# Weight rounding paced by products instead of by turns, with three chunks rounded in earlier turns, in a fused attention and feed-forward kernel

## The chip, the cores and the metric

The kernel runs on one core of a Trainium2 chip. The metric is the device time of one execution in microseconds (us). The engines are named as the profile names them: PE is TensorE (matmuls and transposes), PEld its weight loads, DVE is VectorE, ACT is ScalarE, POOL is GpSimd, SP is SyncE, which issues most DMAs. Each engine works through its own instructions in the order in which the program issues them, and waits at an instruction until what that instruction needs is there.

## The reference

Four batches, eight heads, 768 positions, 64 numbers per head. Every query and every key is assigned to the nearest of 16 centroids of its head; a query attends only to keys of its own cluster. The result goes through a feed-forward block of 512 to 2048 to 512 with a quick GELU.

```python
mask = q_assign[:, :, :, None] == k_assign[:, :, None, :]
scores = np.where(mask, scale * np.matmul(q, k.transpose(0, 1, 3, 2)), -1e9)
attn = softmax(scores)
x = (attn @ v).transpose(0, 2, 1, 3).reshape(B * S, H * D)
h = x @ w_in
out = ((h * (1.0 / (1.0 + np.exp(-1.702 * h)))) @ w_out).astype(np.float32)
```

The attention inputs are 32-bit floats. The two weight matrices come as 64-bit floats, and the chip computes in 32 bits, so the kernel has to round them first. That rounding is what the change moves.

## The kernel before, in words

**Turns.** Attention is cut into 96 turns, counted by t in the loop at L643. A turn works on two key tiles (128 keys against 384 queries, for two heads at a time). Three turns make a group: one pair of heads, one half of the queries. Turns 0 to 23 are batch 0, 24 to 47 batch 1, and so on. In a turn the program issues: the scores on PE (L420); for batch 0 the mask as a second small matmul (L434); the exponentials on ACT (L445); from batch 1 on the mask as a multiplication on DVE (L456, four per turn); the sums of the exponentials on POOL (L469); the products with the values of the turn before on PE (L481). When t leaves the remainder 1 on division by 3 (from turn 4 on) the turn also normalises a group: two PE matmul pairs (L493), then a reciprocal (L496) and a multiplication (L498) on DVE.

**Preparation.** The next head pairs are prepared in pieces that a table hands to turns (L611 to L621): transposes of q and k (`prep_turn`, PE L298, copied out by ACT L303), `prep_near` (PE L312, ACT L318), `prep_assign` (PE L323, then five DVE instructions L329 to L344 or L352), and `prep_hot` in batch 0 (PE L385, then a DVE copy L390 and an ACT copy L392) or `prep_spread` later. `prep_assign(1)`, `(2)` and `(3)` are in turns 1, 3 and 6, `prep_hot(1)`, `(2)` and `(3)` in turns 2, 4 and 7; `prep_assign(4)` is in turn 21 and `prep_assign(5)` in turn 24.

**Three banks.** Most small PE results go to one pool of three PSUM banks (`bank()`, L107, with bufs=3 at L91), handed out in rotation in program order. A fourth request waits until the readers of the first are done. Transposes, `prep_near`, `prep_assign`, `prep_hot` (two banks), the normalisation, and the products of the feed-forward block all ask here; so does a chunk that is rounded in PSUM.

**Rounding.** The weights are 32 chunks of 128x512 64-bit numbers (512 KB each): 16 of w_in, then 16 of w_out. `rounding` (L165) is a generator with four steps, each a DVE instruction: L174, L178, L181 and L185. With the first step it asks for the load of the chunk two further on (`load_w`, an SP DMA, three buffers). With the fourth step it also issues the final addition L189, either on POOL as two halves of 128x256 or on DVE as one instruction of 128x512, and `check_w` on ACT (L219, L222, each with an accumulator read). `step()` runs one step, `round_next()` a whole chunk, `round_to(n)` whatever is missing to n chunks, and `advance(n)` up to n steps as long as the counter `steps[0]` is above 0. The arguments that `round_next` hands on say where the sum is built and which engine adds: `(True, nc.vector)` is in PSUM and on DVE, nothing is in SBUF and on POOL.

**The second block in attention.** After turn 13 the first half of batch 0 is complete, and its feed-forward block is worked off between the turns: 16 products of the first layer (`first`, PE L554, each followed by a tanh on ACT, L517, and a multiplication on DVE, L518, which frees the bank), then 12 of the second (`second3`, PE L527). The counter `owed` (L673 to L691) takes 1.6 products per turn: one in turns 14, 16, 19, 21, 24 and 26, two in the others up to turn 28. I number the first 16 from 0. `first` calls `advance(3)` between its matmuls and its tanh; the loop calls `advance(2)` after every product, `advance(2)` before the masks, `advance(1)` once in the middle and once after every preparation piece.

**Rounding before the change.** One chunk each in turns 0, 2, 5, 8, 9, 11, 12 and 13, in turns 0, 2 and 13 at the end of the turn. From turn 14 on each turn adds 8 steps to the counter.

Of the kernel before, what the change touches and what calls it, by code (L numbers as in the profile page):

```python
# [18 lines left out]
def kernel(  # L19
    tc: tile.TileContext,  # L20
    q: bass.AP,
    k: bass.AP,
    v: bass.AP,
    centroids: bass.AP,
    moe_w_in: bass.AP,
    moe_w_out: bass.AP,
    out: bass.AP,
):

    args = (q, k, v, centroids, moe_w_in, moe_w_out, out)
    bad = fast(tc, *args)
    with tc.If(bad > 0):
        general(tc, *args)
# [3 lines left out]
def fast(  # L39
# [26 lines left out]
    nc = tc.nc  # L66
# [8 lines left out]
    HP = H // 2  # L75
# [123 lines left out]
    def step(*how):  # L199

        if not now and w_done[0] < NW:
            now.append(rounding(*(how or (False, nc.gpsimd))))
        if now:
            n = w_done[0]
            next(now[0])
            if w_done[0] > n:
                now.clear()

    def round_next(*how):
        n = w_done[0]  # L210
        while w_done[0] == n < NW:
            step(*how)
# [201 lines left out]
    def scores(u):  # L414
        g, kt = divmod(u, NJ)
        p, h = split(g)
        ps = ps_s.tile([P, 2, 512], FP32, name="s")
        for a in range(2):
            rows = slice(a * D, (a + 1) * D)
            nc.tensor.matmul(out=ps[:, a, 0:HALF],  # L420
                             lhsT=T[p, 1][rows, kt * P:(kt + 1) * P],
                             rhs=T[p, 0][rows, h * HALF:(h + 1) * HALF],
                             start=True, stop=(p >= HP))
        s_of[u] = ps[:, :, 0:HALF]

    def part(u):

        g, kt = divmod(u, NJ)
        p, h = split(g)
        if p >= HP:  # L430
            return
        for a in range(2):
            r = 32 * (2 * (p % 2) + a)
            nc.tensor.matmul(  # L434
                out=s_of[u][:, a, :],
                lhsT=hots[p // 2, 1][r:r + NC, kt * P:(kt + 1) * P],
                rhs=hots[p // 2, 0][r:r + NC, h * HALF:(h + 1) * HALF],
                start=False, stop=True)

    def exps(u):  # L440
        p, h = split(u // NJ)
        s = s_of[u]
        if p < HP:
            A_of[u] = ap.tile([P, 2, HALF], FP32, name="A")
        nc.scalar.activation(out=A_of[u] if p < HP else s, in_=s, func=AF.Exp,  # L445
                             scale=SCALE)

    def mask(u):

        g, kt = divmod(u, NJ)  # L450
        p, h = split(g)
        s = s_of.pop(u)
        if p >= HP:
            A_of[u] = ap.tile([P, 2, HALF], FP32, name="A")
            for a in range(2):
                nc.vector.scalar_tensor_tensor(  # L456
                    out=A_of[u][:, a, :],
                    in0=qcode[p][:, a, h * HALF:(h + 1) * HALF],
                    scalar=code[p][:, kt % NH, 1, kt // NH, a:a + 1],
                    in1=s[:, a, :], op0=ALU.is_equal, op1=ALU.mult)  # L460
        A = A_of[u]
        if kt == 0:
            return
        if kt == 1:
            sum_of[g] = ap.tile([P, 2, HALF], FP32, name="sum", bufs=2)


        for a in range(2) if w_done[0] < NW else (slice(0, 2),):
            nc.gpsimd.tensor_tensor(  # L469
                out=sum_of[g][:, a],  # L470
                in0=(A_of[u - 1] if kt == 1 else sum_of[g])[:, a],
                in1=A[:, a], op=ALU.add)

    def values(u):
        g, kt = divmod(u, NJ)
        p, h = split(g)
        if kt == 0:
            o_of[g] = ps_o.tile([P, 512], FP32, name="o")
        A = A_of.pop(u)
        for a in range(2):  # L480
            nc.tensor.matmul(out=o_of[g][a * D:(a + 1) * D, 0:HALF],  # L481
                             lhsT=v_in[p][:, a, kt, :], rhs=A[:, a, :],
                             start=(kt == 0), stop=(kt == NJ - 1))
        if kt == NJ - 1:
            O_of[g] = xp.tile([P, HALF], FP32, name="x")
            nc.scalar.copy(O_of[g], o_of.pop(g)[:, 0:HALF])  # L486

    def normalise(g):

        sm = sum_of.pop(g)  # L490
        ps = bank()
        for a in range(2):
            nc.tensor.matmul(out=ps[a * D:(a + 1) * D, 0:HALF], lhsT=twos,  # L493
                             rhs=sm[:, a, :], start=True, stop=True)
        rec = recs[g] = short()
        nc.vector.reciprocal(out=rec, in_=ps[:, 0:HALF])  # L496
        x = xT_of[g] = O_of.pop(g)
        nc.vector.tensor_tensor(out=x, in0=x, in1=rec, op=ALU.mult)  # L498
        if g % HP == HP - 1 and g < 2 * HP:
            (half_ffn, ffn)[g // HP].extend((ffn_half, ffn_tiles)[g // HP]())  # L500
# [3 lines left out]
    def check(g):  # L504


        rec = recs.pop(g)
        nc.scalar.activation(out=rec, in_=rec, func=AF.Copy,
                             accum_out=row_sums[:, 0, g:g + 1])
        nc.scalar.activation(out=rec, in_=rec, func=AF.Relu, bias=top[:, 0:1],  # L510
                             scale=-2.0 * LIMIT * LIMIT,
                             accum_out=row_sums[:, 1, g:g + 1])
# [23 lines left out]
    steps = [0]  # L536

    def advance(n):
        while n and steps[0] > 0:
            step()  # L540
            steps[0] -= 1
            n -= 1
# [65 lines left out]
    TG = NJ // 2  # L608
    TB = 2 * HP * TG

    prep_at = {}  # L611
    for p in range(1, NPAIR):
        b, hp = divmod(p, HP)
        for i in range(2 if p == 1 else 0, len(PREP)):
            if p == 1:
                t = (i - 2) // 2
            elif b == 0:
                t = (hp - 2) * TG + 1 + i // 2
            else:
                t = b * TB + TG * hp - (7, 7, 6, 6, 4, 3, 2)[i]  # L620
# [5 lines left out]
    def prep(p, i):  # L626
        if i == 0 and p:
            load_v(p)
        PREP[i](p)
        if i in (1, 3) and loads:  # L630
            load_qk(*loads.popleft())
# [2 lines left out]

    pace = {t: 1 for t in (0, 2, 5, 8, 9, 11, 12, 13)}
    owed = 0.0
    for p, i in [(0, i) for i in range(6)] + [(1, i) for i in range(2)]:
        prep(p, i)  # L640
# [2 lines left out]
    for t in range(NT + 2):  # L643
        us = range(2 * t, 2 * t + 2) if t < NT else ()
        for u in us:
            scores(u)
        if t == 0:
            prep(0, 6)
        for u in us:
            part(u)  # L650
        for u in us:
            exps(u)
        second_half = t >= TB // 2
        if t > TB // 2 + 1:
            steps[0] += 8
        late = t <= 2 or t == TB // 2 + 1
        if pace.get(t) and not late:
            round_next(*((True, nc.vector) if t > HP * TG // 2 else ()))
        advance(2)
        if recs:  # L660
            check(*recs)
        for u in us:
            mask(u)
        work = sorted(prep_at.get(t, ()), key=lambda w: PREP[w[1]] != prep_near)
        while work and PREP[work[0][1]] == prep_near:
            prep(*work.pop(0))
        if 1 <= t <= NT:
            for u in range(2 * t - 2, 2 * t):
                values(u)

        kept = NF // 2 if t < NT - 3 else NF // 4
        todo = half_ffn or (ffn if len(ffn) > kept else ())
        if not todo:  # L673
            owed = 0.0
        elif half_ffn:
            owed += rate
        else:
            owed += 0.65 if t < NT - 3 else 1.0
        g = (t - 2) // TG if t >= 2 and (t - 2) % TG == TG - 1 else None
        if g is not None and second_half:  # L680
            normalise(g)
        advance(1)
        for p, i in work:
            prep(p, i)
            advance(1)
        if g is not None and not second_half:
            normalise(g)
        while owed >= 1 and todo:
            todo.popleft()()
            owed -= 1  # L690
            advance(2)  # L691
        if pace.get(t) and late:
            round_next(t > 2, nc.vector)
    check(*recs)
    qcode.clear()
    att.close()
# [648 lines left out]
```

## Time and profile before

| what | value |
|---|---|
| median of 6 runs | 1028.02 us (1027.31 to 1030.46) |
| the profiled execution | 1027.92 us, of which the span from first to last instruction is 1026.1 us |
| PE busy | 990.5 us, 97% of the span |
| DVE busy | 676.9 us, 66% |
| POOL busy | 445.2 us, 43% |
| ACT busy | 373.6 us, 36% |
| granted clock of PE, mean | 0.991 |
| turn 0 starts, turn 14 starts, turn 26 starts | 11.12, 75.77, 197.45 us |

The busy shares are means over stages that differ. The change touches turns 0 to 26 alone, the first fifth of the span, so it has to be read there: which engine has no idle time left in a stretch of turns, and which instruction PE waits for.

### The profile page before, as it was taken

The page shows a single profiled execution, that of the slowest core. Times are in us where ns is not written, and L with a number is a line of the kernel's source. Part 1 is how long each engine was busy: PE and PEld are TensorE (multiplying, and loading weights), DVE is VectorE, ACT ScalarE, POOL GpSimd, SP SyncE. Part 2 cuts the span into 40 slices and gives each one's busy share as a digit, 9 for nine tenths or more (in the row PEclk, how much of TensorE's full clock was granted, in tenths as well). Part 3 has the DMA queues.
Part 4 walks back from the last instruction along what each step waited for, and adds up shares of the span by engine and source line. Part 5 has one row for each costly group of instructions (what it writes and reads, how often), then busy time and mean ns, then how long its engine had stood idle before and what let it go on. Part 6 is the DMA issues. An engine that isn't in the chain of part 4 may idle for free.

```text
span 1026.1 us, 12628 instructions
## 1 busy us (share of the span) xinstructions
PE 990.5 (97%) x4574; PEld 580.6 (57%) x4574; DVE 676.9 (66%) x1054; ACT 373.6 (36%) x761; POOL 445.2 (43%) x373
## 2 busy tenths in 40 slices
PE   7999888999999999999999999999999999999997
PEld 3434444344554445543454355688755888656886
DVE  4699999745676877777877677734477535576431
ACT  5677667333455454555444222200122100222000
POOL 3687877623665566556666677400022000120000
PEclk9999999899999999999999999999999999999999
DMA  8413544210022200221000000000000000000000
GB/s 227 129 63 124 170 143 148 74 45 19 1 62 70 71 27 7 56 70 32 19 2 1 11 1 1 0 21 21 21 1 0 1 21 21 21 0 1 21 22 24
DMA packets 66118, 45.25 MB, mean 44 GB/s; under 512 B 52096, under 2 KB 60032, under 8 KB 66048
## 3 DMA queue, kind: packets, MB, share of 16 engines
q1 hardware_dynamic: 65904, 44.33, 14.7%
q8 instruction: 38, 0.62, 0.3%
q14 instruction: 32, 0.26, 0.1%
q10 hardware_dynamic: 144, 0.03, 0.0%
HBM read 38.04 MB, written 6.31 MB: 43 GB/s over the span
## 4 chain that ended last, share of the span: by engine, by line
PE 85%; DVE 11%; ACT 2%; issue 1%; DMA 0%; SPq 0%; DVEq 0%; ACTq 0%
PE b L842 21%; PE b L785 21%; PE s L420 12%; PE o L481 11%; PE m L527 8%; PE m L584 5%; PE m L298 2%; PE m L493 2%; DVE e L185 2%; PE m L554 1%; DVE e L181 1%; DVE short L496 1%; PE m L312 1%; DVE w_in L178 1%; DVE w_out L178 1%
## 5 line engine op out<-in xcount | busy, mean ns | idle before, releaser
L469 POOL TENSOR_TENSOR sum<-sum,A 128x768 f32<-128x768 f32 (+1 forms) x162 | 244.2, 1521 | 126.9 <-DVE A L456 117.1
L456 DVE SCALAR_TENSOR_TENSOR A<-qb,code,s 128x384 f32<-128x384 uint8 x288 | 157.5, 608 | 88.9 <-ACT s L445 53.8
L420 PE MATMUL s<-T,T 64*128 64x384 f32 x768 | 153.0, 511 | 2.3 <-DVE A L456 0.4
L445 ACT ACTIVATE s<-s 128x768 f32<-128x768 f32 x144 | 109.0, 793 | 104.9 <-PE s L420 92.5
L481 PE MATMUL o<-A,inv 128*64 128x384 f32 x768 | 145.1, 499 | 1.1 <-ACT x L486 1.1
L723 POOL TENSOR_TENSOR W<-w_in 128x256 f32<-128x256 f32 x24 | 17.7, 739 | 260.8 <-PE b L785 259.1
L776 DVE TENSOR_TENSOR G<-b,G 128x384 f32<-128x384 f32 x168 | 93.4, 556 | 48.1 <-PE b L785 41.3
L517 ACT ACTIVATE th<-G 128x384 f32<-128x384 f32 x96 | 50.2, 523 | 163.2 <-DVE G L776 102.8
L776 DVE TENSOR_TENSOR y<-b,y 128x256 f32<-128x256 f32 x54 | 22.1, 423 | 130.0 <-PE b L842 93.8
L420 PEld LDWEIGHTS s<-T,T 64*128 64x128 f32 x768 | 65.0, 185 | 74.4 <-issue 33.2
L785 PE MATMUL b<-x,w_in 128*128 128x384 f32 x288 | 101.2, 486 | 0.0
L481 PEld LDWEIGHTS o<-A,inv 128*64 128x64 f32 x768 | 46.6, 136 | 85.2 <-issue 81.5
L469 POOL TENSOR_TENSOR sum<-A 128x768 f32<-128x768 f32 (+1 forms) x41 | 62.0, 1522 | 59.9 <-DVE A L456 34.0
L496 DVE RECIPROCAL short<-m 128x384 f32<-128x384 f32 x32 | 81.6, 2551 | 9.0 <-PE m L493 8.0
L518 DVE SCALAR_TENSOR_TENSOR G<-th,G 128x384 f32<-128x384 f32 x96 | 68.5, 714 | 16.8 <-ACT th L517 14.2
L785 PEld LDWEIGHTS b<-x,w_in 128*128 128x128 f32 x288 | 54.7, 190 | 37.9 <-issue 0.5
L785 PE MATMUL b<-x,W 128*128 128x384 f32 x192 | 70.5, 490 | 0.0
L842 PE MATMUL b<-Z,G 128*128 128x256 f32 x288 | 65.1, 379 | 0.0
L527 PE MATMUL m<-w_out,g 128*128 128x512 f32 x120 | 60.0, 619 | 4.2 <-DVE short L332 3.7
L842 PE MATMUL b<-w_out,G 128*128 128x256 f32 x288 | 63.6, 379 | 0.0
L842 PEld LDWEIGHTS b<-w_out,G 128*128 128x128 f32 x288 | 54.6, 190 | 8.1
L842 PEld LDWEIGHTS b<-Z,G 128*128 128x128 f32 x288 | 54.7, 190 | 7.4
(126 smaller groups left out, 1343.9 us busy)
## 6 DMA issues: line engine op xcount, KB each, us to landing
raw<-in_moe_w_in_dram SPq DMA_DIRECT2D x16, 512.0 KB, 4.7
raw<-in_moe_w_out_dram SPq DMA_DIRECT2D x16, 512.0 KB, 3.4
in<-in_q_dram SPq DMA_DIRECT2D x32, 192.0 KB, 3.6
in<-in_k_dram SPq DMA_DIRECT2D x32, 192.0 KB, 3.0
inv<-in_v_dram SPq DMA_DIRECT2D x16, 384.0 KB, 4.2
out_dram<-y SPq DMA_DIRECT2D x15, 256.0 KB, 2.4
qb<-line SPq DMA_DIRECT2D x12, 192.0 KB, 3.3
out_dram<-y SPq DMA_DIRECT2D x18, 128.0 KB, 1.8
```

What stands on the lines that cost most here:

```text
L420: nc.tensor.matmul(out=ps[:, a, 0:HALF], lhsT=T[p, 1][rows, kt * P:(kt + 1) * P], rhs=T[p, 0][rows, h * HALF:(h + 1) * HALF], start=True, ...
L445: nc.scalar.activation(out=A_of[u] if p < HP else s, in_=s, func=AF.Exp, scale=SCALE)
L456: nc.vector.scalar_tensor_tensor(out=A_of[u][:, a, :], in0=qcode[p][:, a, h * HALF:(h + 1) * HALF], scalar=code[p][:, kt % NH, 1, kt // NH ...
L469: nc.gpsimd.tensor_tensor(out=sum_of[g][:, a], in0=(A_of[u - 1] if kt == 1 else sum_of[g])[:, a], in1=A[:, a], op=ALU.add)
L481: nc.tensor.matmul(out=o_of[g][a * D:(a + 1) * D, 0:HALF], lhsT=v_in[p][:, a, kt, :], rhs=A[:, a, :], start=(kt == 0), stop=(kt == NJ - 1))
L496: nc.vector.reciprocal(out=rec, in_=ps[:, 0:HALF])
L518: nc.vector.scalar_tensor_tensor(out=g, in0=t, scalar=1.0, in1=h, op0=ALU.add, op1=ALU.mult)
L527: nc.tensor.matmul(out=ps[:, 0:DM], lhsT=g, rhs=w_out[:, f, :], start=(f == 0), stop=(f == NF - 1))
L584: nc.tensor.matmul(out=ps[:, f % 2 * P:(f % 2 + 1) * P], lhsT=w_in[:, c, f * P:(f + 1) * P], rhs=xT[c][:, n * P:(n + 1) * P], start=(c == ...
L776: nc.vector.tensor_tensor(out=o, in0=p, in1=a, op=ALU.add)
L785: nc.tensor.matmul(out=ps[:, 0:HALF], lhsT=a[:, c], rhs=x(c), start=(c == 0), stop=(c == 1))
L842: nc.tensor.matmul(out=ps[:, 0:DN], lhsT=a(f // 4)[:, f % 4], rhs=z(f), start=(f == 0), stop=(f == FB - 1))
```

## The change

Rounding before turn 14 covers three more chunks, in turns 1, 3 and 6, at the end of the turn. In turns 0 to 6 all of these now use the default form, with the addition on POOL; before, turns 0 and 2 added on DVE. From turn 14 on the counter no longer takes 8 steps per turn. It takes 4 with every product, at the moment the product is started, and 2 at the start of a turn that doesn't normalise (t % 3 != 1).

```diff
-    pace = {t: 1 for t in (0, 2, 5, 8, 9, 11, 12, 13)}
+    first, last = (5, 8, 9, 11, 12), (0, 1, 2, 3, 6, TB // 2 + 1)
...
         second_half = t >= TB // 2
-        if t > TB // 2 + 1:
-            steps[0] += 8
-        late = t <= 2 or t == TB // 2 + 1
-        if pace.get(t) and not late:
-            round_next(*((True, nc.vector) if t > HP * TG // 2 else ()))
+        dense = t > TB // 2 + 1
+        how = (True, nc.vector) if t > HP * TG // 2 else ()
+        if t in first:
+            round_next(*how)
+        if dense and t % TG != 1:
+            steps[0] += 2
         advance(2)
...
         while owed >= 1 and todo:
+            steps[0] += 4 if dense else 0
             todo.popleft()()
             owed -= 1
             advance(2)
-        if pace.get(t) and late:
-            round_next(t > 2, nc.vector)
+        if t in last:
+            round_next(*how)
```

Here TB is 24, TG is 3 and HP is 4, so `TB // 2 + 1` is turn 13 and `t > HP * TG // 2` means t > 6.

## The prediction

> **What bounds the kernel where the change acts.** I looked first at the busy times by stage, cutting the span where turns begin: turns 8 to 13 (52.6 to 75.8), 14 to 17, 18 to 21, 22 to 24, and 25 to 31. The columns are the length, then the busy time of PE, PEld, DVE, ACT and POOL, the granted PE clock, DMA share and GB/s.
>
> ```profile
> 52.60:75.80 23.20, 21.84 (x131) 8.10 (x130) 21.84 (x23) 18.63 (x42) 20.32 (x21) 1.00 0.22 69
> 75.80:113.50 37.70, 32.94 (x140) 15.56 (x138) 36.63 (x45) 24.56 (x58) 29.73 (x29) 0.95 0.45 138
> 113.50:152.80 39.30, 35.62 (x164) 17.30 (x163) 37.84 (x49) 25.39 (x59) 32.39 (x31) 0.96 0.46 144
> 152.80:186.70 33.90, 30.13 (x127) 14.17 (x126) 31.48 (x43) 19.57 (x46) 23.07 (x24) 0.90 0.50 148
> 186.70:257.60 70.90, 70.66 (x282) 30.61 (x281) 36.47 (x55) 24.75 (x50) 27.66 (x20) 1.00 0.13 37
> ```
>
> From turn 8 to turn 24 DVE is busy 93 to 97% of the time and PE only 87 to 94%; from turn 25 on PE never waits (70.66 of 70.90). So DVE bounds turns 8 to 24 and PE all that follows. The waits of PE in turns 14 to 24 say where DVE makes itself felt (us in total, times, longest):
>
> ```profile
> PE m L554 <- DVE x L518: 4.8, 2, 3.3
> PE m L527 <- DVE short L332: 3.7, 1, 3.7
> PE m L554 <- DVE short L332: 3.5, 1, 3.5
> ```
>
> In order of time: 1.43 in turn 16 (product 3 needs the bank of product 1), 3.34 in turn 17 (product 4, bank of product 3), 3.52 in turn 21 (product 11, bank of `prep_assign(4)`), 3.68 in turn 24 (first product of layer two, bank of `prep_assign(5)`). After 180.56, when the last one ends, PE waits for nothing. **The date of L332 in turn 24 is therefore what the first stage costs.** The third view is DVE's own timeline back from there:
>
> ```profile
> 53.16 2.56 DVE L496 RECIPROCAL short<-m 128x384 f32<-128x384 f32 x1 [0.92 <-ACT qb L392]
> ...
> 147.92 0.56 DVE L332 TENSOR_TENSOR short<-m,best 128x384 bf16<-128x384 f32 x1
> ...
> 156.92 2.56 DVE L496 RECIPROCAL short<-m 128x384 f32<-128x384 f32 x1 [1.37 <-PE m L493]
> ...
> 179.86 0.56 DVE L332 TENSOR_TENSOR short<-m,best 128x384 bf16<-128x384 f32 x1
> ```
>
> Between 53.16 and 180.42 DVE has one pause over 0.15 us, the 1.37 before the reciprocal of turn 22, where it waits for PE. So three links in a row: DVE without pause to L332 of turn 21 (148.48), PE from there to the normalisation of turn 22, DVE without pause to L332 of turn 24.
>
> **What one rounding step costs.** DVE's groups in turns 14 to 24 (busy us, mean ns):
>
> ```profile
> L185 DVE SCALAR_TENSOR_TENSOR e<-raw,e 128x512 f32<-128x512 uint32 x24 | 22.1, 922 | 0.7
> L178 DVE SCALAR_TENSOR_TENSOR w_out<-raw,w_out 128x512 int32<-128x512 int32 x15 | 17.0, 1131 | 0.5
> L181 DVE TENSOR_SCALAR e<-w_out 128x512 int32<-128x512 int32 x14 | 11.0, 784 | 1.1
> L174 DVE TENSOR_SCALAR w_out<-raw 128x512 int32<-128x512 int32 x15 | 10.0, 664 | 0.0
> ```
>
> That is 3.50 per chunk, and 3.38 for the eight w_in chunks: 0.86 per step. It depends on POOL. With POOL idle the four steps of a chunk took 2.25 (84.18 to 86.43); beside POOL's sums they took 4.06 (26.58 to 30.64, in turn 2). The ends for a step are 0.56 and 1.02.
>
> **Part 1: turns 0 to 7.** Each of the three new chunks stands on DVE behind `prep_assign` and ahead of the copy L390 of the next turn's `prep_hot`. In turns 2 and 4 that copy holds a bank that the second transpose of the same turn needs: three banks, `prep_hot` takes two, the first transpose the third. Turn 2 on DVE, then on PE:
>
> ```profile
> 23.88 0.65 DVE L344 TENSOR_TENSOR hot<-code,rank 128x384 bf16<-128x384 f32 x1
> 25.99 0.56 DVE L390 COPY qb<-m 64x768 bf16<-64x768 bf16 x1 [1.47 <-PE m L385]
> ```
>
> ```profile
> 26.22 0.93 PE L298 MATMUL m<-ident,in 128*128 128x128 f32 x6
> ```
>
> The second transpose starts about 26.65, just behind the copy's end at 26.55. With a chunk from 24.53 on, and POOL held by the chunk's own addition (so near the low price, 2.4), the copy runs 26.9 to 27.5: PE waits **0.85** (0.75 at 2.25; 2.5 at 4.06). In turn 4 L344 ends at 34.75 and the transpose starts at 36.3; the copy would end at 37.7, and 0.5 later since POOL, delayed in turn 2, now works beside L335 (1.09 in turn 7 instead of 0.36): **1.9** (1.25 to 3.8). In turn 7 no transpose follows, but DVE's reciprocal does; of the chunk's 2.4 the pauses there swallow 0.61 and 0.92, which leaves DVE **0.8** late (0.7 to 2.5). PE is then 2.75 late and DVE 3.55 (bounds 2.7 and 8.8). As DVE has no pause from 53.16 on, all 3.55 goes into the chain. Nothing excludes that POOL is silent throughout, but a gain there is excluded: the additions that leave DVE in turns 0 and 2 (2 times 0.69) ended before DVE had to wait for PE anyway (4.21 and 0.62).
>
> What else these chunks issue: ACT's `check_w`, 1.7 to 1.8 each, falls into ACT's pauses of 1.29, 1.95 and 1.81 before the exponentials of turns 2, 4 and 7; uncovered it would cost 0.5. Three loads of 512 KB come earlier, where DMA is busy 66% (turns 0 to 4) and 44% (5 to 7); the chunk they load is needed two chunks later. SP's queue has a free buffer each time, so the q and k loads behind are not held up; else PE would wait for them, up to the 3 to 5 us of a load. POOL gets ten more halves by turn 6 and runs some 4 us late in turn 7; the exponentials of turn 9 need its sums, which had 3.9 to spare. I count 0; each us beyond 4 would count one.
>
> **Part 2: turns 14 to 24.** 21 chunks are left instead of 24, so 12 steps fewer, about 10 us of DVE. But they must come off ahead of the two L332 to count. Following the calls of `advance` through the turns gives the steps issued from turn 14 on, before and after the change:
>
> | ahead of | before | after |
> |---|---|---|
> | L518 of product 1 (turn 15) | 14 | 11 |
> | L518 of product 3 (turn 16) | 22 | 19 |
> | L332, turn 21 | 59 | 56 |
> | L496, turn 22 | 66 | 60 |
> | L332, turn 24 | 83 | 80 |
> | end | 96 | 84 |
>
> So 9 of the 12 go away behind the last L332, under PE work that never waits: worth 0 (uncovered they would be 7.7). To L332 of turn 21: 3 steps fewer, **-2.6** (-1.7 to -3.1). To the reciprocal of turn 22 PE leads, which keeps the -2.6; the 3 further steps saved here only lengthen DVE's pause. From there to turn 24's L332 it is 17 steps before and 20 after: **+2.6** (1.7 to 3.1). Sum 0, within 1.4 either way. Other order changes (steps ahead of a gelu, POOL's L189 ahead of sums in turns 15, 18, 21 and 24) move a step's mean price; 0.04 on 56 steps is 2.2 either way.
>
> [...] Matmuls after waits of 3.34 to 3.68 run slow (eight L554 take 4.21 after the wait of turn 21 and 2.85 after the 1.43 of turn 16; sixteen take 7.12 in turn 17 and 5.43 in turn 20), and the clock in these stages is 0.90 to 0.96. [...] L174 takes 0.41 to 1.22. [...]
>
> **Sum.** 3.55 + 0 = 3.55 on the profiled execution's 1027.92 (0.10 below the median of the runs): 1031.5 us.
>
> **Rivals.** *Even* (0.22): POOL is silent beside the new chunks (+2.7) and turn 21's wait falls low enough to leave the matmuls at speed (4.21 to 2.85, -1.4): 1029.2. For it: the low price was measured; against: turn 21's bank is freed no sooner relative to PE. *Faster* (0.16): DVE's backlog, not its total, is the trouble. With each gelu 1 to 8 steps nearer its product, steps get cheaper, and the waits of turns 16, 17 and 21 vanish (-8.3) with two slow stretches (-1.7, -1.4): 1027.9 + 3.6 - 11.4 = 1020.1. It needs a mean step under 0.76 in turns 14 to 21 (5.7 us more off 56 steps). For it: 0.56 is possible; against: POOL's work there is the same. *Dearer* (0.10): the new chunks run beside POOL's sums (8.8): 1036.7, or 1038.4 if turn 4's wait then slows the matmuls as turn 17's did (7.12 less 5.43). That the steps don't come as planned is excluded by the count: `round_to` never finds a chunk missing.
>
> **Chances.** The forecast's own case has 0.52 (1030 to 1034). About 0.2% (2 us) is what a measurement of this kernel can tell from no change. Slower 0.62 (forecast and dearer), same 0.22, faster 0.16. The range, 1025 to 1036.5, leaves out most of *faster* and half of *dearer*.
>
> **What would show it.** Right: PE waits before L298 for DVE's L390 in turns 2 and 4 (0.85, 1.9); turn 14 starts near 78.5; the wait before L527 in turn 24 grows to about 6; turn 26 starts near 201; no wait in turn 16. Wrong: no L390 wait (part 1), or turn 24's L332 earlier than 182 (part 2: the price of a step).

## The result and the profile after

The changed kernel takes 1028.08 us (median of 37 runs) where the kernel before takes 1029.3 us (75 runs, among them later ones than the six of the prediction). The ratio is 0.9986, with a 95% interval of 0.9982 to 0.9991: faster by about 1.4 us. I had forecast 3.5 us slower, and had put at 2 us what can be told from no change; over this many runs 1.4 is clear of the noise. The profiled execution has a span of 1025.3 us against 1026.1.

First the busy times of the changed kernel by stage, cut at the same turns as before (length; PE, PEld, DVE, ACT, POOL; PE clock, DMA share, GB/s):

```profile
56.43:80.46 24.03, 22.00 (x129) 8.26 (x129) 22.96 (x27) 18.86 (x42) 22.32 (x22) 1.00 0.28 88
80.46:117.33 36.87, 32.92 (x140) 15.60 (x138) 35.69 (x43) 23.03 (x54) 29.83 (x29) 0.95 0.43 134
117.33:156.53 39.20, 35.41 (x162) 17.28 (x161) 37.30 (x46) 23.80 (x55) 31.74 (x31) 0.96 0.49 150
156.53:184.98 28.45, 27.66 (x125) 13.23 (x124) 24.65 (x34) 19.34 (x46) 20.74 (x22) 1.00 0.43 123
184.98:255.95 70.97, 70.73 (x282) 30.66 (x281) 36.79 (x56) 23.14 (x46) 25.70 (x16) 1.00 0.13 37
```

The stages from turn 8 to turn 21 are as long as before, within 0.9 us. The turns ahead of them are longer: turn 8 starts at 56.43 instead of 52.56, with turn 0 at 11.15 and 11.12. The gain is in the fourth line: turns 22 to 24 take 28.45 instead of 33.90, and PE's clock there is 1.00 instead of 0.90. What PE waits for, up to turn 26 (us in total, times, longest):

```profile
...
PE m L554 <- DVE x L518: 3.9, 1, 3.9
PE m L298 <- DVE qb L390: 3.2, 2, 2.3
PE m L554 <- DVE short L332: 2.9, 1, 2.9
...
PE m L527 <- ACT T L303: 0.6, 1, 0.6
```

The two waits for L390 are new and are those I had forecast, 0.91 and 2.25. The wait of turn 16 is gone, also as forecast. But the wait of 3.68 before L527 for L332 in turn 24, which I had forecast to grow to 6, is missing. PE in that turn, before and after, and DVE after:

```profile
180.56 2.04 PE L527 MATMUL m<-w_out,g 128*128 128x512 f32 x2 [3.68 <-DVE short L332]
182.40 4.33 PE L527 MATMUL m<-w_out,x 128*128 128x512 f32 x6
```

```profile
181.35 1.13 PE L527 MATMUL m<-w_out,g 128*128 128x512 f32 x2 [0.64 <-ACT T L303]
182.31 2.74 PE L527 MATMUL m<-w_out,x 128*128 128x512 f32 x6
```

```profile
184.89 0.56 DVE L332 TENSOR_TENSOR short<-m,best 128x384 bf16<-128x384 f32 x1
```

The product starts at 181.35 and L332, for which it had waited before, runs only at 184.89. The product no longer needs the bank that L332 reads. The built programs list a bank for every tile: of the 201 requests to the three-bank pool the first 78 get the same bank in both kernels, and then they part, exactly at this product.

```
request, turn             before  after
76  prep_assign(5)  24       0      0
77  transpose       24       1      1
78  transpose       24       2      2
79  product (L527)  24       0      1
80  normalisation   25       1      2
81  prep_spread     25       2      0
82  prep_near       26       2      0
83  transpose       26       1      2
84  transpose       26       2      0
```

So the banks are not handed out in strict rotation, as I had written; the tile framework chooses them when the kernel is built, and the changed rounding, the only thing that differs, was enough to change its choice. That became the theory: **the gain is the other bank, and the rounding itself costs about what it saves.** The rival: the pacing made the gain, as the diff suggests. To separate them, the runs below hand out the banks from a list. The edit is the same in all of them, with the digits of the one or the other program ("old banks", "new banks"):

```diff
-    ps_m = ctx.enter_context(tc.tile_pool(name="ps_m", bufs=3, space=PS))
+    ps_m = [ctx.enter_context(tc.tile_pool(name=f"ps_m{i}", bufs=1, space=PS)) for i in range(3)]
...
-        return ps_m.tile([P, 512], FP32, name="m")
+        return ps_m[banks.popleft()].tile([P, 512], FP32, name="m")
```

### The profile page after: what moved, and what is told of

Read it like the earlier page. It is cut to its first block, busy times and chain, and to the rows that moved or that the text cites. A ratio compares the mean times of both kernels' runs of the same rounds, so it can differ in the third digit from the quotient of the medians.

```text
span 1025.3 us, 12630 instructions
## 1 busy us (share of the span) xinstructions
PE 989.2 (96%) x4574; PEld 579.6 (57%) x4574; DVE 676.0 (66%) x1052; ACT 373.2 (36%) x761; POOL 446.5 (44%) x375
## 4 chain that ended last, share of the span: by engine, by line
PE 84%; DVE 12%; ACT 2%; issue 1%; DMA 0%; POOL 0%; DVEq 0%; ACTq 0%
PE b L844 21%; PE b L787 21%; PE s L420 11%; PE o L481 10%; PE m L527 8%; PE m L584 5%; DVE e L185 2%; PE m L298 2%; PE m L493 2%; DVE e L181 1%; PE m L554 1%; DVE short L496 1%; PE m L312 1%; DVE w_out L178 1%; DVE w_out L174 1%
## 5 line engine op out<-in xcount | busy, mean ns | idle before, releaser
L527 PE MATMUL m<-w_out,g 128*128 128x512 f32 x120 | 59.1, 611 | 1.1 <-ACT T L303 1.1
```

Source lines behind the costliest of these rows:

```text
L527: nc.tensor.matmul(out=ps[:, 0:DM], lhsT=g, rhs=w_out[:, f, :], start=(f == 0), stop=(f == NF - 1))
```

## Experiments

**1. The changed kernel with old banks.**

> The changed kernel, with the PSUM banks of the small pool handed out as in the kernel before. Theory (bank): the changed kernel gained only because the first product of layer two in turn 24 came to lie in the bank of a transpose instead of that of prep_assign(5). Put back, PE waits in turn 24 for DVE's L332 again, about 4.7 us (185.45 less 180.71), and its matmuls run slow after it, about 2.1 to 2.7 more: turn 25 starts about 7 us later than in the changed kernel, and the kernel takes about 1035 us, slower than before. Rival (pacing): the steps tied to products made the gain; then turn 24 stays as in the changed kernel and the time at about 1028.

Measured: 1034.83 us, ratio 1.0057 (1.0044 to 1.0070). PE in turn 24:

```profile
186.92 2.05 PE L527 MATMUL m<-w_out,g 128*128 128x512 f32 x2 [4.88 <-DVE short L332]
188.76 3.91 PE L527 MATMUL m<-w_out,x 128*128 128x512 f32 x6
```

The wait is back (4.88), the eight matmuls take 5.75 instead of 3.70, and turn 25 starts 14.70 after turn 24 instead of 8.41. In this run 122 further requests have another bank than in the changed kernel. But from turn 10 to the end of attention no other turn differs from the changed kernel's by more than 0.25, so it is this bank that counts, and handing out from a list costs nothing that shows. (Turns 4 to 9, ahead of the first other bank, differ by 0.6 in sum; see the last section.) The theory holds: without the other bank the change is a loss of nearly 6 us.

**2. The kernel before with new banks.**

> The kernel before, with the banks handed out as in the changed kernel; nothing of the rounding is changed. Theory (bank): in turn 24 the wait of 3.68 for L332 goes, a short one for ACT's copy stays (about 1.3), the matmuls run at speed; turn 25 starts 4 to 5 us sooner and the kernel takes 1024 to 1025.5 us. Rival (pacing): no effect, 1029, since the rounding still falls due by turn.

Measured: 1028.45 us, ratio 0.9990 (0.9981 to 0.9998). Half a miss. Turn 24 shrinks as expected, from 13.92 to 9.10, with a wait of 1.33 for ACT. But turn 26 grows from 8.05 to 10.49: PE waits 2.32 for ACT's L318, and ACT had been stuck (PE's wait first, then ACT):

```profile
PE m L298 <- ACT short L318: 2.3, 1, 2.3
```

```profile
195.94 0.71 ACT L219 ACTIVATE raw<-raw 128x512 f32<-128x512 f32 x1 [6.99 <-DVE w_out L178]
...
200.21 0.46 ACT L318 COPY short<-m 128x384 f32<-128x384 f32 x1
```

This is `check_w` of the last chunk. It alone writes its result over the raw chunk (the others use the tile of the last chunk as scratch), so ACT waits until DVE has read the raw data in L178; behind it stand the exponentials, the checks L508 and L510 and the copy L318, whose bank a transpose of turn 26 needs. With PE early, the rounding that is left late does have a price. (In this profile turns 21 and 22 are also longer, by 1.26 and 0.3; see the last section.)

**3. and 4. Each half of the change alone, old banks.** The edits against the changed kernel (3) and against the kernel before (4):

```diff
-        if dense and t % TG != 1:
-            steps[0] += 2
+        if dense:
+            steps[0] += 8
...
-            steps[0] += 4 if dense else 0
```

```diff
-        if t > TB // 2 + 1:
-            steps[0] += 8
+        dense = t > TB // 2 + 1
+        if dense and t % TG != 1:
+            steps[0] += 2
...
+            steps[0] += 4 if dense else 0
             todo.popleft()()
```

> Only the first half of the change: the three early chunks (and the additions of turns 0 and 2 on POOL), 8 steps per turn from turn 14 on, banks as before. Theory: PE waits before L298 for L390 in turns 2 and 4 as in the changed kernel (0.9 and 2.3), turn 14 starts 4.7 us late, 83 steps stand ahead of turn 24's L332 as before, so its date is about 5 us late, and nothing gives this back: about 1034 us. Rival (the early chunks relieve the dense turns): turn 24's L332 no later than before, 1029 or less.

> Only the second half of the change: 8 chunks before turn 14 as before, 24 after it, 4 steps per product and 2 per turn that does not normalise, banks as before. Theory: turn 14 starts as before; 80 steps instead of 83 ahead of turn 24's L332, which comes 0 to 2.6 us sooner; PE still waits for it, 3.5 us or more, and runs slow after it: 1027 to 1029 us. Rival (pacing): the waits of turns 16, 17, 21 and 24 shrink together, 1024 us or less.

Measured: 3 has a ratio of 1.0061 (1.0048 to 1.0074), about 6 us slower, as the theory said; the wait of turn 24 is 3.65. 4 takes 1035.9 us, ratio 1.0071 (1.0058 to 1.0084), which neither side expected. Its turn 24 is as expected (wait 4.91), but turn 26 takes 13.68 instead of 8.05. PE's waits from there on:

```profile
PE m L527 <- POOL w_out L189: 3.2, 2, 2.8
```

Without the early chunks the slower pacing issues 88 steps to the end of turn 25, not 96. That leaves two chunks over (I had counted three), and the products of turn 26 need them. So the two halves belong together: the early chunks cover what the pacing leaves over.

**5. and 6. Each half alone, new banks.** The same edits.

> The early chunks with 8 steps per turn as before, and the changed kernel's banks. Theory (banks and early chunks give the gain, the pacing little): the wait for L332 in turn 24 goes as in the changed kernel, 5 to 6 us less than with the old banks, about 1030; the last chunk is checked in turn 24, so ACT waits for DVE there and not in turn 26. Rival (the pacing matters as much): 1032 or more, since 83 steps instead of 80 stand ahead of the same places.

> The pacing alone, without the early chunks, and the changed kernel's banks. Theory: the wait for L332 in turn 24 goes (about 5 us less than with the old banks), but at the end of turn 25 three chunks are still unrounded, so the products of turn 26 wait for POOL's L189 as in the run with the old banks (turn 26 lasts over 13 us instead of 8): 1031 to 1034 us. Rival (three early chunks are not needed): turn 26 lasts 8 us, 1026.

Measured: the early chunks alone 1030.36 us, ratio 1.0013 (1.0004 to 1.0023); the pacing alone 1030.78 us, 1.0016 (1.0007 to 1.0025), just under the range given; its turn 26 takes 14.71 (again two chunks, not three, were left). With the other results this fills a table (ratio to the kernel before):

| | old banks | new banks |
|---|---|---|
| rounding as before | 1 | 0.9990 |
| early chunks alone | 1.0061 | 1.0013 |
| pacing alone | 1.0071 | 1.0016 |
| both (the change) | 1.0057 | 0.9986 |

In every row the new banks are the better ones, with the change by 0.7%. In the right column the change and the rounding as before have overlapping intervals: what the diff does on purpose is worth nothing that can be measured there, and costs 0.57% with the old banks. In the same column each half alone is slower than both together, and slower than the rounding as before.

**7. The chunks of turns 1, 3 and 6 ahead of the preparation pieces (new banks).** They stood on DVE between `prep_assign` and L390; here they come first.

```diff
-    first, last = (5, 8, 9, 11, 12), (0, 1, 2, 3, 6, TB // 2 + 1)
+    first, last = (5, 8, 9, 11, 12), (0, 2, TB // 2 + 1)
...
+        if t in (1, 3, 6):
+            round_next()
         advance(1)
         for p, i in work:
```

> The changed kernel with its own banks, but the chunks of turns 1, 3 and 6 stand ahead of the preparation pieces of their turn instead of behind them, where DVE sat idle for 4.2, 0.6 and 4.2 us. Theory (the chunks cost because L390 stands behind them): the waits of 0.91 in turn 2 and 2.6 in turn 4 go, or shrink to under 1 together, turn 14 starts 2.5 to 4 us sooner than in the changed kernel, and all later turns with it: 1024 to 1026 us. Rival (the chunks cost by their amount of work on DVE, POOL and ACT, wherever they stand): turn 14 no sooner, 1028.

Measured: 1027.26 us, ratio 0.9979 (0.9970 to 0.9988); expected were 1024 to 1026. This interval overlaps that of the change (0.9982 to 0.9991), so no gain over the changed kernel is shown. The waits for L390 are gone, but turn 4 has a new one, for the end of `prep_assign(2)`:

```profile
42.09 1.05 PE L385 MATMUL m<-ident_h,hot 128*64 128x128 bf16 x12 [4.44 <-DVE hot L344]
```

In turn 3 the new chunk queues behind that of turn 2 (eight steps without pause from 28.99 to 38.34), and `prep_assign(2)` behind both. In turns 1 and 6 nothing was lost. Counted from turn 0, turn 14 starts 1.3 later than in the changed kernel instead of 2.5 to 4 sooner. So neither side was right: here a chunk was free only where DVE's pause was long enough for it (in the kernel before DVE pauses 4.21 ahead of L329 in turns 1 and 6, and 0.62 in turn 3).

**8. As 7, with two more banks exchanged.** Product 4 gets the bank of the first transpose of turn 17 instead of product 3's, product 11 that of the first transpose of turn 21 instead of `prep_assign(4)`'s; all later banks are renamed to fit.

> As the run with the chunks ahead of the preparation pieces, and also products 4 and 11 get the bank of a transpose instead of that of product 3 and of prep_assign(4). Theory (PE waits for DVE only through the bank that it is handed): the waits of 3.95 in turn 17 and 2.9 in turn 21 go with the slow matmuls after them (1.7 and 1.4), but as DVE's own work is not less, part comes back as waits for DVE elsewhere, at the latest where the second layer needs its last rounded chunks in turn 26: 3 to 8 us less than that run, 1017 to 1023 us. Rival (DVE's total is the bound up to turn 24): the waits only move to the next bank, and the time stays within 1.5 us of that run.

Measured: 1025.64 us, ratio 0.9968 (0.9958 to 0.9979): 1 to 2 us better than 7, not 3 to 8. The waits of turns 17 and 21 shrink to 1.55 and 1.07 (for ACT), but turn 18 gets one of 2.70 for a gelu:

```profile
PE m L554 <- DVE x L518: 2.7, 1, 2.7
PE m L554 <- ACT T L303: 2.6, 2, 1.5
PE m L298 <- DVE x L518: 1.5, 2, 1.1
```

From turn 16 to turn 25 it is 86.78 instead of 89.35. That is nearer to the rival: DVE's total work bounds these turns (from 75 to 205 DVE is busy 116.60 of 130.00), and a better bank mostly moves the wait.

**9. The kernel before, with other banks for the three products that wait in turns 17, 21 and 24.**

> The kernel before with its rounding untouched, but products 4 and 11 and the first product of layer two in turn 24 get the bank of a transpose. Theory: the three waits of 3.34, 3.52 and 3.68 go or shrink, yet DVE and POOL finish the last of the 24 chunks about 199 us into the span as before, and the product of turn 26 that needs it started at about 201: so most of the gain turns into a wait for POOL's L189 in turn 25 or 26, and 2 to 4 us are left: 1025 to 1027.5 us. Rival (banks alone explain all of it): 1018 to 1022 us without the change's early chunks.

Measured: 1029.25 us, ratio 1.0001 (0.9992 to 1.0010). That is above both ranges given. Counted from turn 0, turn 25 starts 5.7 us sooner than before, and turn 26 gives it all back (14.17 instead of 8.05). That most of it would turn into another wait was right, the place wrong: it is not POOL but ACT, which here sits 9.0 at the check of the last chunk.

```profile
PE m L298 <- ACT short L318: 4.3, 1, 4.3
```

**10. As 8, with the third chunk at the end of turn 4 instead of in turn 3.**

```diff
-    first, last = (5, 8, 9, 11, 12), (0, 2, TB // 2 + 1)
+    first, last = (5, 8, 9, 11, 12), (0, 2, 4, TB // 2 + 1)
...
-        if t in (1, 3, 6):
+        if t in (1, 6):
```

> As the run with free banks, but the third chunk is rounded at the end of turn 4, behind the normalisation, instead of in turn 3 ahead of prep_assign(2); those of turns 1 and 6 stay ahead of the preparation pieces. Theory (a chunk is free where DVE waits for PE anyway: 4.2 us in turn 1, 1.6 and 4.2 around turns 5 and 6): the wait of 3.53 before L385 in turn 4 goes, at most 1 us comes back in turn 7: 2.5 to 4 us less than that run, 1022 to 1023.5 us. Rival (the time is set later, by DVE's backlog in turns 14 to 24): turn 14 starts sooner but turn 25 does not, 1025.5.

Measured: 1023.08 us, ratio 0.9937 (0.9924 to 0.9951), as expected and better than both kernels. (The profiled execution was the fastest of the six, 1020.07.) The wait of turn 4 is gone, and one of 2.49 before L385 in turn 7 has come, more than the 1 us I allowed:

```profile
PE m L298 <- DVE x L518: 2.8, 3, 1.1
PE m L554 <- DVE x L518: 2.7, 1, 2.7
PE m L385 <- DVE hot L344: 2.5, 1, 2.5
```

Turn 5 now starts at 37.98, where it was 37.72 before and 41.44 in the changed kernel.

## Why the prediction was wrong

*The step that failed* is "The date of L332 in turn 24 is therefore what the first stage costs". It took for granted that the product of turn 24 lies in the bank of `prep_assign(5)` after the change too. The changed rounding gave it another bank (the table of requests): PE waited 0.64 there, not 6, and turn 24 took 8.41 instead of 13.92. Experiment 1 puts the old bank back and shows a loss of the kind that I had forecast, with 4.88 of wait and a ratio of 1.0057, 5.9 us where my sum was 3.55. In its profile turn 25 starts 111.06 after turn 14, before 110.89, so with the old banks the 0 of part 2 held and what is missing lies in part 1. Nothing in the profile of before showed a bank number, and I counted banks by a rule that I had not checked.

*DVE's dates* were roughly right. L332 of turn 24 ended at 185.45; the prediction implies 183.97 (180.42 plus 3.55). That is in part luck: at L332 of turn 21 DVE was 2.8 later than forecast, and from there to turn 24 it lost 1.3 where 2.6 were forecast.

*Part 1* was right in mechanism and nearly in size: 0.91 and, with 0.35 before L385, 2.60 against 0.85 and 1.9. DVE's own steps in turn 2 beside an idle POOL, whose pause of 2.76 ends at 27.13 (columns: start, length):

```profile
24.71 0.43 DVE L174 TENSOR_SCALAR w_in<-raw 128x512 int32<-128x512 int32 x1
25.17 0.69 DVE L178 SCALAR_TENSOR_TENSOR w_in<-raw,w_in 128x512 int32<-128x512 int32 x1
25.90 0.43 DVE L181 TENSOR_SCALAR e<-w_in 128x512 int32<-128x512 int32 x1
26.36 0.69 DVE L185 SCALAR_TENSOR_TENSOR e<-raw,e 128x512 f32<-128x512 uint32 x1
27.08 0.56 DVE L390 COPY qb<-m 64x768 bf16<-64x768 bf16 x1
```

That is the low price, 2.37 from the first step to the copy. The other two new chunks were dearer, 3.12 in turn 4 and 3.23 in turn 7, where 2.4 was assumed. None of the three reached the upper price of 4.06. Turn 14 started 4.7 late, not 2.75. Of the missing 2, about 0.8 are the larger waits of turns 2 to 4 (0.91 and 2.60 against 2.75 in all), and another 0.8 comes in turns 9 and 10. There ACT's check L508 waits 0.57 for a late L498 and holds up the exponentials, and PE then waits 0.83 for them; the sum had no term for this path.

*Part 2*: the table of steps held. The 2.6 ahead of turn 21's L332 came out smaller (that instruction was 3.7 late, not 0.95): DVE entered turn 14 5.2 late, not 3.55, and the three steps bought 1.5. A rounding step cost what I had assumed (3.4 per chunk), but the multiplication L498 of turns 16 and 19 took 1.33 and 1.30, before 0.70 and 0.68, which takes away the difference.

*"9 of the 12 go away behind the last L332 ... worth 0"* is true only as long as PE is held up in turn 24. Once it is not, what is left of the rounding decides turn 26: through ACT's last check (experiments 2 and 9) or through unrounded weights (4 and 6). This is what the early chunks buy. Together with the pacing it pays for what they cost in turns 2 to 10; with 8 steps per turn it does not (1.0013 against 0.9990 with the new banks).

*The rivals*: none was the one that came. "Faster" had the right sign for a wrong reason: the waits of turns 17 and 21 did not vanish (3.95 and 2.87), and the mean step did not get cheaper. "Even" lay nearest in time (1029.2), by terms that did not come: turn 14 was 4.7 late, not 2.7, and turn 21 took 12.50 against 12.60.

What stays open: by which rule the framework chose the other bank. No run varied that.

## What to carry to other kernels

A pool that several stages share ties them together by which buffer each gets, and a reordering can change that far from the edit: compare the buffers of the two built programs before a gain or a loss is put down to the order itself. Work that fills an engine's pauses is free only where the pause stands in the queue ahead of the instruction that others wait for, so look for the pause first and place the work in it (in experiment 7 the chunks of turns 1 and 6 cost nothing, that of turn 3 a wait of 4.44). When a wait is removed, price the next thing that was hidden behind it; here it was the check of the last chunk on a third engine, ACT, which waited 6.99 there in experiment 2.

## What the runs showed of the hardware

*The slow stretch after a wait depends on more than the wait's length.* In the changed kernel and in experiment 1 PE waits the same 2.25 in turn 4. Turns 4 and 5 then take 12.81 at a clock of 1.00 and 14.40 at 0.88 (length; busy times; clock):

```profile
32.80:45.61 12.81, 10.21 (x70) 4.72 (x69) 10.74 (x13) 6.68 (x13) 9.81 (x11) 1.00 0.46 126
```

```profile
33.36:47.76 14.40, 11.80 (x70) 5.23 (x69) 10.98 (x14) 6.70 (x13) 9.81 (x11) 0.88 0.43 135
```

Before and in experiment 2 PE waits 3.52 and 3.53 in turn 21; the turn takes 12.60 and 13.86, with a clock of 0.86 and 0.78. A wait of 2.70 in turn 18 left the clock at 0.88 in experiment 8 and at 1.00 in experiment 10:

```profile
114.64:128.63 13.99, 11.29 (x44) 5.67 (x43) 13.02 (x17) 6.57 (x15) 12.27 (x13) 0.88 0.66 197
```

```profile
111.35:123.64 12.29, 9.59 (x43) 4.88 (x42) 11.87 (x16) 6.58 (x15) 11.20 (x11) 1.00 0.77 222
```

So a wait of 2.25 or of 2.70 was followed by a lower clock in one run and not in another; what decides it, no run here shows.

*Whole profiles differ behind the attention, and by their start.* Behind the attention PE waits 2.5 to 2.6 once in every profile; in those of the two kernels the clock from 586 to 589, shortly after it, is 0.61 (before) and 0.54 (after). From turn 95 to the end it takes 460.0 in experiments 1, 7 and 10, and 461.4 to 461.9 in the other nine profiles. By my estimate from these clocks, those 3 us cost 1.2 to 1.4; that the three shorter profiles are without them is not shown. Turn 0 starts between 11.1 and 13.3, and no chunk is rounded ahead of it. So single profiles are compared here by the lengths of turns, and whole times by the ratios of many runs.
